# Another order for the pairs of the inverse transform, and the first weight split on GpSimd, in a spectral filter and MLP kernel

## The chip, the cores and the metric

The kernel runs on one core of a Trainium2 chip. The metric is the time of one execution on the device in microseconds (us). A core has TensorE (PE, with PEld for the loads of its stationary operand), VectorE (DVE), ScalarE (ACT), GpSimd (POOL) and SyncE (SP), which issues the DMAs here. Each engine takes its own instructions in program order; semaphores hold an instruction until what it needs is done.

## The reference

A block of a GFNet with an MLP, on 2048 tokens of 576 channels, all in float32:

```python
def _A_ref(x, w_r, w_i):                  # S = 2048, D = 576
    X = jnp.fft.rfft2(x, axes=(-2, -1))
    X = X * (w_r + 1j * w_i)
    return jnp.fft.irfft2(X, s=(S, D), axes=(-2, -1))

def _B_ref(x, w1, w2):                    # w1 576 x 4608, w2 4608 x 576
    h = jnp.maximum(jnp.einsum("bsd,df->bsf", x, w1), 0)
    return jnp.einsum("bsf,fd->bsd", h, w2)

h  = x + _A_ref(layernorm(x), w_r, w_i)
h2 = h + _B_ref(layernorm(h), w1, w2)
```

## The kernel before, in words

The tokens lie in 16 tiles t of 128 rows. The kernel goes through four stages.

1. The forward transform: layer norm (`stat1`, `norm1`), `fold` over the channels, and `fwd_a`, tile after tile.
2. The middle: for 16 groups of frequencies, `mid_d` finishes the forward transform over the channels, `mid_b` transforms over the tokens and multiplies with the filter, `mid_i` begins the way back and writes its result to the buffer `U`. In the middle the first weights of the MLP are read from memory (`load_weights(0)`: a block of `w1` and a block of `w2`).
3. The inverse, interleaved with the first pieces of the MLP. This is the loop over u, a *round* for each pair of tiles, that the change reorders.
4. The main loop: the rest of the MLP as a list of `steps` (g, c), each a group g of 256 hidden units by a chunk c of 4 tiles. From step 8 on the second product is done in Winograd form (`slot`, `prod`, `add`, line 601 and 608).

All products are float32 made of rounded parts: `split` makes a high part h (`act`, a rounding copy on ACT, line 151) and a low part l = v - h (line 307), and a product adds h x h, h x l and l x h. The weights of group 0 go through `split_weights(0, 0)` (`w1`, 1280 columns) and `split_weights(0, 1)` (`w2`, 1152 columns).

The functions of a round, by what they do on which engine:

- `inv_h(u)`: `left` for the two new tiles 2u, 2u+1 (TensorE, into a fresh PSUM buffer each) and `row` for the two old tiles 2u-2, 2u-1 (TensorE, reads `inv_y` in `U`), then line 443 adds the old tiles' result to `xs`, on DVE.
- `inv_d(t)`: four matmuls in `left`'s buffer, an ACT copy into an `e` buffer `ez`, DVE at lines 461 and 462, then the two halves of `inv_y(t)`: line 464 on GpSimd, line 465 on DVE.
- `stat2(t)`: `ln_stats` on the finished tile: lines 208 and 209 on DVE, then for each pair lines 211, 212 and 214 on GpSimd.
- `norm2(t0, 2)`: line 222 on ACT writes the normalized pair `z`.
- `project(t)`: five transposes of `z` on TensorE (lines 483 and 484), two copies on ACT, then the low parts: line 493 on GpSimd, line 494 on DVE. The result goes to the token buffers `xc`, which the MLP's first product reads.
- `unit(k)`: a quarter of an MLP step. Quarters 0 and 1 are `mm1` (first product, 14 matmuls of 512 columns each; after the second, lines 518 and 519 make the split hidden block on ACT and DVE), quarters 2 and 3 are two `mm2` each (second product, 12 matmuls of 288 columns; line 536 adds the result to `xs` on DVE). Units 10 and 11 hold a quarter of step 3's `mm1` as well.

Line 148 is the matmul of nearly all of these, so the profile's rows are told apart by tile names and sizes: `d` is PSUM, `e` the shared buffers, `X` is `U` (later the buffer `tail`), `A` is `xs`, `B`, `C` are `xc`, `D` the hidden blocks.

Nothing schedules this by cost: the order is written out by hand, and each engine follows it. Two shared stocks tie the pieces together beyond their data. There are four PSUM buffers, taken by `left`, `row`, `project`, `mm1` and `mm2` in turn, and ten `e` buffers, taken by `ez`, by `project`, by `z`, by the raw weights (two a group), by the constants `c3t` and by the split weights (two to four a group). A taker gets the buffer that has been free for longest and waits until its last reader is done.

In the order before, round u runs `inv_h(u)`, `norm2` of the pair of round u-2, `inv_d` of pair u, `stat2` of pair u-1, then `project` of the pair just normalized, and in rounds 3 to 8 two units that may read that same pair. `split_weights(0, ...)` stands in rounds 1 and 2.

Of the kernel before, what the change touches and what calls it, by code (L numbers as in the profile page):

```python
# [11 lines left out]
F32R = mybir.dt.float32r  # L12
# [6 lines left out]
NT = 16  # L19
# [102 lines left out]
def dims(ap, off, *pairs):  # L122

    return bass.AP(tensor=ap.tensor, offset=ap.offset + off, ap=[list(ap.ap[0]), *[list(p) for p in pairs]])
# [3 lines left out]
def kernel(ctx: ExitStack, tc: tile.TileContext, x, w_r, w_i, w1, w2, cc2, c1, fb, ib, c3, out):  # L128
    nc = tc.nc
# [3 lines left out]
    def sb(shape, tag, bufs=1, dt=F32):  # L133
        n[0] += 1
        return pool.tile(shape, dt, tag=tag, name=f"{tag}_{n[0]}", bufs=bufs)

    n = [0]

    def ps():
        n[0] += 1  # L140
        return psum.tile([128, 1024], F32, tag="d", name=f"d_{n[0]}", bufs=4)

    def ebuf(shape, dt=F32):
        e = sb([128, EW], "e", EB, dt)[:, :int(np.prod(shape[1:]))]
        return e.rearrange("p (a b) -> p a b", a=shape[1]) if len(shape) == 3 else e

    def mm(o, l, r, start, stop):
        nc.tensor.matmul(o, l, r, start=start, stop=stop)  # L148

    def act(o, i, **kw):  # L150
        nc.scalar.activation(o, i, AF.Copy, **kw)  # L151
# [65 lines left out]
    def ln_apply(xs, t0, k, mvr, zs):  # L217

        r = mvr[2]
        for i in range(k):  # L220
            yield
            nc.scalar.activation(zs[i], xs[:, t0 + i, :], AF.Identity, bias=r[:, 2, i:i + 1], scale=r[:, 1, i:i + 1])  # L222
# [73 lines left out]
    def load_weights(g):  # L296
        v1, v2 = ebuf([128, 5, 256]), ebuf([128, 2, D])
        f = slice(256 * g, 256 * g + 256)
        nc.sync.dma_start(v1[:, 0:4], w1[0:512, f].rearrange("(a p) f -> p a f", p=128))
        for h in range(2):  # L300
            nc.sync.dma_start(v1[64 * h:64 * h + 64, 4], w1[512:576, f])
        nc.sync.dma_start(v2, w2[f, :].rearrange("(a p) d -> p a d", p=128))
        raw[g] = (v1, v2)

    def split(h, l, v):
        act(h, v)
        nc.vector.tensor_sub(l, v, h)  # L307

    pieces = []

    def work(k):
        for _ in range(k):
            split(*pieces.pop(0))

    def split_weights(g, part):
        if g == 1 and part == 0:
            h, l = tail[0][:, 4608:5888], tail[0][:, 5888:7168]
        else:
            h, l = (ebuf([128, (1280, 1152)[part]], F32R) for _ in range(2))
        h, l = (v.rearrange("p (a n) -> p a n", a=(5, 2)[part]) for v in (h, l))  # L320
        wts[g, part] = h, l
        for k in range((5, 2)[part]) if g >= 2 else [slice(None)]:
            pieces.append((h[:, k], l[:, k], raw[g][part][:, k]))
        if g <= 2:
            work(len(pieces))

    tail = []
# [66 lines left out]
    def rows(t, j):  # L394
        k = 64 * (j ^ t % 2)
        return slice(k, k + 64)
# [10 lines left out]
    xc = [xc01[:, 0], xc01[:, 1], xc2]  # L407
    pds, Ez = {}, {}

    def inv_y(t):  # L410
        return U[:, 640 * t:640 * t + D]

    def inv_h(u):

        new = [2 * u, 2 * u + 1] if 2 * u < NT else []
        old = [2 * u - 2, 2 * u - 1] if u else []
        pa = {}

        def left(t):
            pds[t] = ps()  # L420
            for r in range(2):
                for m in range(2):
                    mm(pds[t][64 * m:64 * m + 64, 512 * r:512 * r + 290],
                       U[64 * r:64 * r + 64, 640 * t + 512 + 64 * m:640 * t + 576 + 64 * m], lpv[64 * r:64 * r + 64, r], True, False)

        def row(k):
            for j in range(2):
                for t in old:
                    h = j ^ k
                    mm(pa[t][rows(t, j), 512 * h:512 * h + 288], cai[64 * j:64 * j + 64, 64 * j:64 * j + 64],  # L430
                       inv_y(t)[64 * j:64 * j + 64, 288 * h:288 * h + 288], True, True)

        for t in new[:1]:
            left(t)
        for t in old:
            pa[t] = ps()
        row(0)
        for t in new[1:]:
            left(t)
        row(1)  # L440
        for t in old:
            xt = xs[:, t, :].rearrange("p (h n) -> p h n", h=2)
            nc.vector.tensor_add(xt, xt, pa[t].rearrange("p (h n) -> p h n", h=2)[:, :, :288])  # L443

    def inv_d(t):
        pd = pds.pop(t)
        ut = [dims(U, 640 * t + 128 * b, [1, 128]) for b in range(4)]
        for r in range(2):
            o = pd[:, 512 * r:512 * r + 290]
            for h in range(2):  # L450
                mm(o[:, 145 * h:145 * h + 145], ut[2 * ((r + h) % 2) + r], dev[:, 2 * r + h], False, h == 1)
        if t % 2 == 0:
            Ez[t // 2] = ebuf([128, 4 * 289])
        ez = Ez[t // 2][:, 578 * (t % 2):578 * (t % 2) + 578]
        pdv = pd.rearrange("p (r n) -> p r n", r=2)
        e0, e1 = ez[:, :289], ez[:, 289:578]
        R2 = [289, 2]
        pa_, pb_ = pdv[:, :, 0:145], pdv[:, :, 145:290]
        ea = dims(ez, 0, R2, [1, 145])
        act(ea, pa_)  # L460
        nc.vector.tensor_sub(dims(ez, 288, R2, [-1, 144]), ea[:, :, :144], pb_[:, :, :144])  # L461
        nc.vector.tensor_add(ea, ea, pb_)  # L462
        y = inv_y(t)
        nc.gpsimd.tensor_sub(dims(y, 575, [-1, 287]), e0[:, 1:288], e1[:, 1:288])
        nc.vector.tensor_add(y[:, 0:289], e0, e1)  # L465
# [3 lines left out]
    def stat2(t):  # L469
        t0 = t - t % 2  # L470
        stats[t0] = ln_stats(xs, t0, 2, t % 2, stats.get(t0))

    def norm2(t0, k):
        z = ebuf([128, 2, D])
        for i in range(k):
            Zs[t0 + i] = z[:, i, :]
        return ln_apply(xs, t0, k, stats.pop(t0), [z[:, i, :] for i in range(k)])

    def project(t):
        y = Zs.pop(t)  # L480
        pz = ps()
        for b in range(4):
            nc.tensor.transpose(pz[:, 128 * b:128 * b + 128], y[:, 128 * b:128 * b + 128], ident)  # L483
        nc.tensor.transpose(pz[:, 512:640], y[:, 448:576], ident)
        q = slice(128 * (t % CH), 128 * (t % CH) + 128)
        dst = xc[t // CH]
        pzv = pz.rearrange("p (a s) -> p a s", s=128)
        act(dst[:, 0:5, q], pzv[:, :5])
        if t % 2 == 0:
            Ez[t] = ebuf([128, 1024])  # L490
        zt = Ez[t - t % 2][:, 512 * (t % 2):512 * (t % 2) + 512]
        act(zt, pz[:, :512])
        nc.gpsimd.tensor_sub(dst[:, 5:9, q], zt.rearrange("p (a s) -> p a s", s=128), dst[:, 0:4, q])  # L493
        nc.vector.tensor_sub(dst[0:64, 4, q], pzv[64:128, 4], dst[64:128, 4, q])  # L494
# [65 lines left out]
    def wino_w(*names):  # L560
        for n in names:
            split(*wform(n), fs[n])
# [54 lines left out]
    def slot(i):  # L617
# [16 lines left out]
        add(i, 0, (0, 0))  # L634
        prod(i, "A12", "B21", 1, True)
        split(*fs["S12f"], fs["S12"])
        add(i, 1, (0, 0))
        if w1:
# [41 lines left out]
    def unit(k):  # L680
        i, q = divmod(k, 4)
        if q < 2:
            mm1(i, q)
        else:
            if i == 2:
                mm1(3, q - 2)
            mm2(i, 2 * q - 4)
            mm2(i, 2 * q - 3)

    for u in range(NT // 2 + 2):  # L690
        inv_h(u) if u <= NT // 2 else None
        if 2 <= u:
            for _ in norm2(2 * u - 4, 2):
                pass
        if 2 * u < NT:
            inv_d(2 * u)
            inv_d(2 * u + 1)
        if 1 <= u <= NT // 2:
            stat2(2 * u - 2)
            stat2(2 * u - 1)  # L700
        if u in (1, 2):
            split_weights(0, u - 1)
        if u == 7:
            load_weights(1)
            tail.append(sb([128, 10240], "X", dt=F32R))
            xc.append(tail[0][:, :4608].rearrange("p (a n) -> p a n", a=9))
        if u == 8:
            split_weights(1, 0)
            split_weights(1, 1)
        if u >= 2:  # L710
            project(2 * u - 4)
            project(2 * u - 3)
        if 3 <= u < 9:
            unit(2 * u - 6)
            unit(2 * u - 5)
    for i in range(3, len(steps)):
        if i + 5 < len(steps) and steps[i + 5] == (steps[i + 5][0], 0):
            load_weights(steps[i + 5][0])
# [46 lines left out]
```

## Time and profile before

| | us |
|---|---|
| median of three runs | 1091.26 (1090.89 to 1092.81) |
| the profiled execution | 1092.21 |
| its span, first to last instruction | 1090.1 |
| TensorE busy in the span | 1037.6 (95%) |
| DVE busy | 749.4 (69%) |
| ACT busy | 391.9 (36%) |
| GpSimd busy | 328.7 (30%) |
| mean granted TensorE clock | 0.981 |

The profile is of one execution. A row of the timeline gives start, length, engine, line, operation, what it writes and reads, and in brackets how long the engine stood idle before it and what ended that. A row by stretches gives the stretch, its length, then for PE, PEld, DVE, ACT and POOL the busy time with the number of instructions, then the granted TensorE clock, the busy share of the DMA engines and GB/s. The time of an engine that is not awaited by anyone costs nothing.

### The profile page before, as it was taken

How to read it: one execution, taken by the hardware profiler on the slowest of the kernel's cores; microseconds unless marked ns; L12 is line 12 of the kernel's file. 1: busy time of each engine (PE TensorE's matmuls, PEld its weight loads, DVE VectorE, ACT ScalarE, POOL GpSimd, SP SyncE). 2: the span in 40 equal slices, each digit the busy share in tenths (PEclk: the TensorE clock that was granted, in tenths of full speed). 3: DMA queues.
4: the chain of work that ended last, by engine and by line, in shares of the span. 5: the costliest groups of instructions: out<-in, count | busy, mean ns of one | idle time of the engine just before them, and what ended most of it. 6: DMA issues, size and time to landing. Idle time of an engine off the chain costs nothing.

```text
span 1090.1 us, 17543 instructions
## 1 busy us (share of the span) xinstructions
PE 1037.6 (95%) x6688; PEld 918.6 (84%) x6688; DVE 749.4 (69%) x1411; ACT 391.9 (36%) x894; POOL 328.7 (30%) x436
## 2 busy tenths in 40 slices
PE   8999866969999999999999999999999999999996
PEld 7787545749999999999999999999999999999995
DVE  7587646443447777777777777777777777777765
ACT  4534223232113334333333433333343333334331
POOL 4200244231113243333324323332432333243221
PEclk9999989879999999999999999999999999999998
DMA  9931700101100100000010000001000000100024
GB/s 236 245 78 58 164 1 1 46 12 35 47 20 6 45 24 25 23 25 23 25 46 22 26 22 25 23 25 46 23 26 22 25 23 25 47 23 1 1 71 104
DMA packets 32611, 48.08 MB, mean 44 GB/s; under 512 B 3472, under 2 KB 23184, under 8 KB 32528
## 3 DMA queue, kind: packets, MB, share of 16 engines
q1 hardware_dynamic: 32528, 46.96, 16.0%
q8 instruction: 53, 0.87, 0.3%
q14 instruction: 30, 0.25, 0.1%
HBM read 42.23 MB, written 4.72 MB: 43 GB/s over the span
## 4 chain that ended last, share of the span: by engine, by line
PE 91%; DVE 5%; POOL 2%; ACT 1%; issue 1%; DMA 0%; SPq 0%; DVEq 0%; ACTq 0%; POOLq 0%
PE d L148 58%; PE d L601 32%; DVE st L208 1%; DVE e L462 1%; DVE X L465 1%; DVE e L461 0%; POOL B L493 0%; POOL r L212 0%; ACT e L222 0%; DVE D L519 0%; ACT D L518 0%; DVE mv L209 0%; DMA X<-in_A_x_dram 0%; DVE A L443 0%; PE d L483 0%
## 5 line engine op out<-in xcount | busy, mean ns | idle before, releaser
L608 DVE TENSOR_TENSOR A<-A,d 128x576 f32<-128x576 f32 x448 | 334.6, 747 | 50.1 <-PE d L601 50.0
L601 PE MATMUL d<-X,D 128*128 128x288 f32 x2304 | 346.2, 294 | 1.5 <-DVE A L608 0.9
L601 PEld LDWEIGHTS d<-X,D 128*128 128x128 f32 x2304 | 328.9, 188 | 17.2 <-DVE A L608 1.1
L148 PE MATMUL d<-B,e 128*128 128x512 f32 x952 | 242.4, 396 | 13.8 <-POOL B L493 11.2
L148 PEld LDWEIGHTS d<-B,e 128*128 128x128 f32 x952 | 175.2, 192 | 43.8 <-POOL B L493 11.8
L576 DVE SCALAR_TENSOR_TENSOR D<-d,D 128x256 fp32r<-128x256 f32 x192 | 81.5, 424 | 121.8 <-ACT D L575 121.8
L575 ACT ACTIVATE D<-d 128x256 fp32r<-128x256 f32 x192 | 73.4, 382 | 239.7 <-PE d L148 239.7
L590 POOL TENSOR_TENSOR e<-e 128x256 f32<-128x256 f32 x64 | 47.4, 740 | 355.6 <-ACT e L589 355.6
L148 PE MATMUL d<-C,e 128*128 128x512 f32 x476 | 121.2, 395 | 6.9 <-POOL C L493 5.6
L148 PE MATMUL d<-X,e 128*128 128x512 f32 x476 | 118.8, 390 | 0.0
L151 ACT ACTIVATE X<-e 128x288 fp32r<-128x288 f32 (+2 forms) x177 | 70.2, 434 | 105.6 <-PE d L601 105.6
L307 DVE TENSOR_TENSOR D<-e,D 128x512 fp32r<-128x512 f32 (+1 forms) x128 | 92.7, 724 | 20.0 <-ACT D L151 20.0
L148 PEld LDWEIGHTS d<-C,e 128*128 128x128 f32 x476 | 87.4, 191 | 21.7 <-POOL C L493 5.9
L586 POOL TENSOR_TENSOR e<-e 128x256 f32<-128x256 f32 x64 | 47.5, 742 | 173.4 <-ACT e L585 173.4
L148 PEld LDWEIGHTS d<-X,e 128*128 128x128 f32 x476 | 85.9, 188 | 13.7
L151 ACT ACTIVATE D<-e 128x512 fp32r<-128x512 f32 (+1 forms) x128 | 66.7, 521 | 75.6 <-POOL e L591 71.9
L307 DVE TENSOR_TENSOR X<-e,X 128x288 fp32r<-128x288 f32 (+2 forms) x177 | 83.2, 493 | 0.0
L601 PEld LDWEIGHTS d<-X 128*128 128x128 f32 x384 | 58.0, 188 | 5.1 <-DVE A L608 0.2
L601 PE MATMUL d<-X 128*128 128x288 f32 x384 | 61.4, 295 | 0.0
L519 DVE SCALAR_TENSOR_TENSOR D<-d,D 128x1024 fp32r<-128x1024 f32 x8 | 9.8, 1224 | 65.3 <-ACT D L518 65.3
L148 PE MATMUL d<-e,D 128*128 128x288 f32 x384 | 53.5, 297 | 0.8 <-DVE B L494 0.4
L148 PEld LDWEIGHTS d<-e,D 128*128 128x128 f32 x384 | 52.4, 190 | 1.9 <-DVE B L494 0.6
(79 smaller groups left out, 1015.6 us busy)
## 6 DMA issues: line engine op xcount, KB each, us to landing
e<-in_B_w_dram SPq DMA_DIRECT2D x18, 576.0 KB, 3.8
e<-in_B_w_dram SPq DMA_DIRECT2D x18, 512.0 KB, 3.7
A<-in_A_x_dram SPq DMA_DIRECT2D x16, 288.0 KB, 9.2
out_dram<-A SPq DMA_DIRECT2D x64, 72.0 KB, 2.1
X<-in_A_x_dram SPq DMA_DIRECT2D x12, 288.0 KB, 7.5
e<-in_B_w_dram SPq DMA_DIRECT2D x36, 64.0 KB, 3.5
B<-in_A_w_r_dram SPq DMA_DIRECT2D x15, 144.5 KB, 7.7
B<-in_A_w_i_dram SPq DMA_DIRECT2D x15, 144.5 KB, 7.2
```

Source lines behind the costliest of these rows:

```text
L148: nc.tensor.matmul(o, l, r, start=start, stop=stop)
L151: nc.scalar.activation(o, i, AF.Copy, **kw)
L208: nc.vector.bn_stats(st[:, i, h, :], xs[:, t0 + i, 288 * h:288 * h + 288])
L307: nc.vector.tensor_sub(l, v, h)
L462: nc.vector.tensor_add(ea, ea, pb_)
L465: nc.vector.tensor_add(y[:, 0:289], e0, e1)
L575: nc.scalar.activation(h, p, AF.Relu)
L576: nc.vector.scalar_tensor_tensor(l, p, 0.0, h, op0=ALU.max, op1=ALU.subtract)
L586: nc.gpsimd.tensor_sub(fs["S3"], fs["p0"][:, 0], fs["p0"][:, 1])
L590: nc.gpsimd.tensor_add(fs["S1"], fs["p0"][:, 1], fs["p1"][:, 1])
L601: nc.tensor.matmul(P[:, tt], l[:, q], r, start=first and n_ == 0, stop=n_ == 2, skip_group_check=not first)
L608: nc.vector.tensor_add(xt, xt, P)
```

## The change

Four things are reordered, and one operation moves to another engine. No arithmetic is added or left out.

- The splits of group 0's weights are issued between the middle and round 0, and their low parts are computed by GpSimd instead of DVE. They were in rounds 1 and 2.
- In `inv_h` both `left` stand ahead of all rows; the second stood between the two rows.
- In a round, `project` comes after `inv_d` and takes the pair normalized in the round before (tiles 2u-6, 2u-5, in rounds 3 to 10); `stat2` and then `norm2` follow it. `norm2` stood ahead of `inv_d`, and `project` behind `stat2`. The loop has one round more.
- The units move two rounds on, to rounds 5 to 10, so that a unit reads tokens projected in an earlier round. `load_weights(1)` stays in round 7 but now stands ahead of `project` and `stat2`; `tail` is taken in round 8; the two splits of group 1 fall in rounds 8 and 9 and no longer both in 8.

```diff
-    def split(h, l, v):
+    def split(h, l, v, eng=nc.vector):
         act(h, v)
-        nc.vector.tensor_sub(l, v, h)
+        eng.tensor_sub(l, v, h)
...
-        if g <= 2:
+        if g == 0:
+            split(*pieces.pop(), eng=nc.gpsimd)
+        elif g <= 2:
             work(len(pieces))
...
-        for t in new[:1]:
+        for t in new:
             left(t)
         for t in old:
             pa[t] = ps()
-        row(0)
-        for t in new[1:]:
-            left(t)
-        row(1)
+        for k in range(2):
+            row(k)
...
-    for u in range(NT // 2 + 2):
-        inv_h(u) if u <= NT // 2 else None
-        if 2 <= u:
-            for _ in norm2(2 * u - 4, 2):
-                pass
+    for part in range(2):
+        split_weights(0, part)
+    for u in range(NT // 2 + 3):
+        if u <= NT // 2:
+            inv_h(u)
         if 2 * u < NT:
             inv_d(2 * u)
             inv_d(2 * u + 1)
+        if u == 7:
+            load_weights(1)
+        if u == 8:
+            tail.append(sb([128, 10240], "X", dt=F32R))
+            xc.append(tail[0][:, :4608].rearrange("p (a n) -> p a n", a=9))
+        if 3 <= u:
+            project(2 * u - 6)
+            project(2 * u - 5)
         if 1 <= u <= NT // 2:
             stat2(2 * u - 2)
             stat2(2 * u - 1)
-        if u in (1, 2):
-            split_weights(0, u - 1)
-        if u == 7:
-            load_weights(1)
-            tail.append(sb([128, 10240], "X", dt=F32R))
-            xc.append(tail[0][:, :4608].rearrange("p (a n) -> p a n", a=9))
-        if u == 8:
-            split_weights(1, 0)
-            split_weights(1, 1)
-        if u >= 2:
-            project(2 * u - 4)
-            project(2 * u - 3)
-        if 3 <= u < 9:
-            unit(2 * u - 6)
-            unit(2 * u - 5)
+        if 2 <= u < NT // 2 + 2:
+            for _ in norm2(2 * u - 4, 2):
+                pass
+        if u in (8, 9):
+            split_weights(1, u - 8)
+        if 5 <= u:
+            unit(2 * u - 10)
+            unit(2 * u - 9)
```

## Prediction

> **What bounds the kernel now.** I read the page first, then busy time by stretches, then the waits of TensorE in the stretch that stood out, then the timeline there. From the page, the span and the 40 slices:
>
> ```profile
> span 1090.1 us, 17543 instructions
> PE   8999866969999999999999999999999999999996
> PEclk9999989879999999999999999999999999999998
> ```
>
> TensorE is full from slice 10 on. The holes, and the low clocks, lie in slices 4 to 9, which is the inverse with its interleaved MLP units. Busy time by stretches (us, then each engine's busy time, clock, DMA):
>
> ```profile
> 116.05:127.30 11.25, 9.67 (x89) 6.25 (x89) 5.57 (x12) 2.26 (x5) 2.20 (x3) 1.00 1.05 220
> 134.09:146.80 12.71, 8.26 (x59) 5.39 (x60) 7.95 (x18) 6.54 (x11) 6.71 (x8) 0.87 0.00 0
> 146.80:149.38 2.58, 1.25 (x12) 1.01 (x11) 2.44 (x7) 2.25 (x5) 1.33 (x2) 1.00 0.00 0
> 177.27:182.72 5.45, 5.45 (x59) 4.19 (x58) 3.58 (x7) 1.34 (x3) 0.85 (x2) 1.00 0.00 0
> 182.72:190.16 7.44, 0.50 (x3) 0.19 (x2) 3.58 (x11) 1.77 (x4) 5.31 (x8) 0.73 0.00 0
> 190.16:199.40 9.24, 9.24 (x27) 7.08 (x27) 0.00 (x0) 0.00 (x0) 0.00 (x0) 0.66 0.00 0
> 116.05:257.82 141.77, 106.17 (x721) 82.00 (x721) 69.69 (x146) 43.41 (x69) 47.60 (x62) 0.88 0.16 39
> 257.82:1090.10 832.28, 821.59 (x4835) 745.01 (x4833) 597.21 (x1050) 297.90 (x712) 260.76 (x322) 1.00 0.10 29
> ```
>
> From 116.05 us (first `left`) to 257.82 us (first product of the main loop) TensorE idles 141.77 - 106.17 = 35.6 us, and part of its 106.17 is slow clock: 27 products took 9.24 us at 0.66 where the loop's 28 take 6.47 (below). After 257.82 nothing is left to win: 821.59 of 832.28 is busy. Who held TensorE in the bad stretch (us, times, longest):
>
> ```profile
> PE d L148 <- POOL B L493: 11.2, 2, 5.6
> PE d L148 <- POOL C L493: 5.6, 1, 5.6
> PE d L148 <- DVE X L307: 2.6, 1, 2.6
> ```
>
> L493 writes the last part of a projected token block: three times a pair's first product waits for the projection of its own round. That projection is late because GpSimd first does the statistics (L211 to L214) and because the round's `norm2` stands before it.
>
> **The change, part by part.** I number rounds by u and date each by the first `inv_d` matmul on TensorE. These timeline rows (start, length) show the chain of rounds 1 and 2, then the costs used below:
>
> ```profile
> 114.71 0.90 ACT L151 ACTIVATE X<-d 128x160 f32<-128x160 f32 x4 [2.37 <-PE d L148]
> 118.55 0.41 ACT L151 ACTIVATE e<-d 128x290 f32<-128x290 f32 x1 [2.94 <-PE d L148]
> 121.43 0.90 POOL L464 TENSOR_TENSOR X<-e 128x287 f32<-128x287 f32 x1 [0.45 <-DVE e L462]
> 123.99 2.90 PE L148 MATMUL d<-e,X 128*128 128x145 f32 x24
> 125.73 0.46 DVE L461 TENSOR_TENSOR e<-e,d 128x288 f32<-128x288 f32 x1 [0.63 <-ACT e L151]
> 126.59 1.26 ACT L151 ACTIVATE e<-e 128x1280 fp32r<-128x1280 f32 x1
> 127.32 0.67 PE L148 MATMUL d<-X,cc 64*64 64x288 f32 x2 [0.43 <-DVE X L465]
> 128.06 0.46 DVE L465 TENSOR_TENSOR X<-e 128x289 f32<-128x289 f32 x1
> 128.17 0.90 POOL L464 TENSOR_TENSOR X<-e 128x287 f32<-128x287 f32 x1 [0.45 <-DVE e L462]
> 128.44 0.81 DVE L208 BATCH_NORM_STATS2 st<-A 128x6 f32<-128x288 f32 x2
> 130.21 0.21 DVE L209 BATCH_NORM_AGGREGATE mv<-st 128x2 f32<-128x12 f32 x1
> 130.39 1.49 DVE L307 TENSOR_TENSOR e<-e,e 128x1280 fp32r<-128x1280 f32 x1
> 130.52 1.45 POOL L211 TENSOR_SCALAR r<-mv 128x2 f32<-128x2 f32 x1 [1.44 <-DVE mv L209]
> 130.73 2.25 PE L148 MATMUL d<-e,X 128*128 128x145 f32 x16
> 131.80 1.41 DVE L443 TENSOR_TENSOR A<-A,d 128x576 f32<-128x576 f32 x2
> 135.28 1.16 ACT L151 ACTIVATE e<-e 128x1152 fp32r<-128x1152 f32 x1
> 139.73 1.34 DVE L307 TENSOR_TENSOR e<-e,e 128x1152 fp32r<-128x1152 f32 x1
> 152.88 2.48 POOL L493 TENSOR_TENSOR B<-e,B 128x512 fp32r<-128x512 f32 x2
> 163.37 0.72 PE L148 MATMUL d<-e,X 64*64 64x290 f32 x8
> 163.91 0.67 PE L148 MATMUL d<-X,cc 64*64 64x288 f32 x8
> 164.53 1.22 DVE L519 SCALAR_TENSOR_TENSOR D<-d,D 128x1024 fp32r<-128x1024 f32 x1 [12.61 <-ACT D L518]
> 165.81 0.72 PE L148 MATMUL d<-e,X 64*64 64x290 f32 x8 [1.24 <-DVE D L519]
> 173.54 0.50 DVE L494 TENSOR_TENSOR B<-d,B 64x128 fp32r<-64x128 f32 x2
> 234.53 1.20 PE L148 MATMUL d<-X,cc 64*64 64x288 f32 x16
> 257.82 6.62 PE L148 MATMUL d<-B,X 128*128 128x512 f32 x28
> 264.29 6.54 PE L148 MATMUL d<-e,D 128*128 128x288 f32 x48
> ```
>
> *First weights split at the middle's end.* Two ACT copies (1.26 and 1.16) start after the middle's last copy, at 114.71 + 0.90 = 115.6, and end at 118.0, inside the 2.94 us for which ACT waited before 118.55: nothing. DVE loses its two L307 (1.49 and 1.34). GpSimd gains two subtractions, which no row shows at this size; nearest is L493, 2.48 for two of 512 columns, 1.24 each. Scaled by columns that is 3.1 + 2.8 = 5.9; with a start-up share taken out, as L464's 0.90 for 287 suggests (0.34 for 225 more columns, 1.5 ns each), 2.4 + 2.2 = 4.6. I take 5.5, nearer the rows of like type. They run from 116.9 to 122.4, and both L464 of round 0 are queued behind them: the second ends at 122.4 + 1.8 = 124.2 where it ended at 122.33. So 1.9 us later, between 1.0 and 2.3. If DVE's L465 (both operands in SBUF) shuts GpSimd out, as L307 did to L211 (1.45 for two columns, ending at 131.97, just after L307), two times 0.46 come on top; if it is DVE that is held, about as much.
>
> [...]
>
> *Both `left` ahead of the rows.* From the end of the second L464 (128.17 + 0.90 = 129.07) to `inv_d` at 130.73 are 1.66 us; the second `left` in it takes 163.91 - 163.37 = 0.54, and now lies in the idle time before. So 1.12 remains. All four PSUM buffers are then taken in the order left, left, row, row: behind a unit of first products, the one that waits for L519 is the second row instead of the second `left` (1.24 before; I take 1.3, between 0 and 1.8).
>
> *Rounds 1 to 4, now without units.* Round 1: 124.2 + 1.1 = 125.3 (before 123.99). From `inv_d` to the end of the second L464 are 129.07 - 123.99 = 5.08, so a round takes 5.08 + 1.12 = 6.2 by that chain. DVE needs 1.42 (L443) + 2.79 (125.73 to 128.52) + 1.97 (128.44 to 130.42) = 6.2, and with the projection's L494 (0.50) 6.7. GpSimd needs less than the 6.71 of 134.09:146.80, which is one round of it with an L211 held by the L307 that goes; its statistics now stand behind L493, but only the next round's `norm2` needs them. ACT's `norm2` no longer stands before the next `ez` copies. Rounds: 125.3, 131.5, 137.7, 144.1, 150.8. Round 3 to 4 is a mean of the two pitches.
>
> *Rounds 5 to 10: TensorE full.* Every unit reads tokens projected a round earlier (L493 of round 4 ends at 150.8 - 1.12 + 2.48 = 152.2, the first product starts at 154), every transpose a `norm2` of the round before. A full round is 5.45 of inverse work (2.10 of it before `inv_d`) and 6.47 of first products or 6.38 of second (257.82 to 264.29, and to 270.67). DVE then needs at most 6.7 + 4 x 0.75 = 9.7 in 11.9: covered. Ends:
> - 5: 150.8 + 3.35 + 6.47 = 160.6
> - 6: + 5.45 + 1.3 (L519) + 6.38 = 173.7
> - 7: + 5.45 + 6.47 = 185.6
> - 8: + 1.20 rows + 1.25 project + 6.38 + 0.6 = 195.0; the 0.6 is the second projection's PSUM buffer, which L519 frees late
> - 9: + 1.25 + 6.47 + 0.4 = 203.1; the 0.4 is a buffer freed by the second products' add, behind L307 of group 1
> - 10: + 1.25 + 12.85 = 217.2
>
> The main loop starts at 217.2 instead of 257.82: 40.6 us earlier, of which 1.3 us was given to GpSimd's split. Moving the four weight DMAs of `load_weights(1)` within round 7 costs nothing: SyncE's queue holds nothing else there, and the `e` buffers they take come free in round 6; if they came two rounds late, the split in round 8 would wait. The two splits of group 1 (ACT 1.26 and 1.16, DVE 1.49 and 1.34) now fall in rounds 8 and 9, not both before the first product that needs them; that wait of 2.6 (L307) goes.
>
> The profiled execution took 1092.21, its span 1090.1, and the median of the three runs is 0.95 lower. 1092.21 - 40.6 = 1051.6, less 0.95 is 1050.7. I say **1051**.
>
> **Rivals.**
>
> *The bare rounds cool TensorE (1058).* The clock fell where it idled: 0.87 in 134.09:146.80 (65% busy), 0.66 behind an idle stretch of 5.6. Rounds 1 to 4 fill 4.2 to 5.5 of 6.2 to 6.7. For: that is not full. Against: 116.05:127.30 held 1.00 at 86%, and no wait in rounds 1 to 4 is longer than about 1.3. Price: at 0.75 the 3.2 us of TensorE in each chain grow by 1.1, four times, and the first 27 products by up to 9.24 - 6.24 = 3.0: 7 us.
>
> [...]
>
> *The wait moves to the statistics (1066).* They are queued behind L493 now; if `norm2` were late by those 2.48 in each of rounds 5 to 10, 15 us come back. For: in round 3 the products waited for just this queue, the other way round. Against: `norm2` has a round of 11.9 us to be done.
>
> *It doesn't do what it says (1075).* If a unit waited for any projection into its buffer, rounds 5 and 7 would keep waiting 5.6 each and cool after it, and 9 too: 3 x (5.6 + 2.4) = 24. Against: the rows of a pair's first block start at 127.32, before the second block's L465 and L464 write the same buffer, so regions are told apart.
>
> *Slower (1096).* Weight halves hold four `e` buffers from 116 on, `c3` one, and `z` now lives across rounds: four are left for three takes a round. If each take waited for the round before to end, rounds would run one after the other, at 12.71 + 0.5 as in 134.09:146.80. Eleven of these are 145 instead of 141.77, 4 us slower; it decides from 12.9 a round. Against: each slot is taken again a round or more after its last reader.
>
> **How the numbers follow.** Forecast 0.66, cool rounds 0.18, statistics 0.09, unchanged waits 0.04, slower 0.03. The forecast's own span is 1046 (no stalls in rounds 6 to 9, GpSimd quick) to 1056; with the cooling rival the range is 1046 to 1064, which leaves out some 0.16. About 0.2% is what a measurement can tell from no change: faster 0.96, same 0.01, slower 0.03.
>
> **What would show it.** After: no TensorE wait on L493; L464 of round 0 near 124; `inv_d` pitch 6 to 7 us four times; TensorE full from about 150; the main loop's first product near 217; clock 1.00 throughout. Wrong if the clock dips in rounds 1 to 5, if transposes wait for L222, or if the loop after 217 no longer takes 832 us.

## The result, and the profile after

| | before | after |
|---|---|---|
| median of six executions each, us | 1092.61 | 1054.49 (1052.18 to 1055.34) |
| ratio of the times | | 0.965, 95% interval 0.9636 to 0.9664 |
| profiled execution, us | 1092.21 | 1052.18 |
| its span, us | 1090.1 | 1050.3 |

The kernel is 38 us faster; the forecast was 1051, within 1046 to 1064. The page of the changed kernel, span and slices:

```profile
span 1050.3 us, 17539 instructions
PE   8999899999999999999999999999999999999995
PEclk9999999999999999999999999999999999999998
```

Of the dent in slices 4 to 9 only the 8 in slice 4 is left, which holds round 0; the low clocks there are gone. Busy time by stretches (stretch, length, then PE, PEld, DVE, ACT, POOL, clock, DMA), cut at the first `inv_d` of rounds 1, 2 and 3, then rounds 5 and 6, then the sums that answer to those of before:

```profile
116.04:125.74 9.70, 6.77 (x66) 3.96 (x65) 5.29 (x7) 2.58 (x4) 7.25 (x4) 1.00 1.05 222
125.74:131.99 6.25, 5.57 (x50) 3.45 (x49) 5.39 (x14) 0.83 (x2) 1.80 (x2) 1.00 0.55 117
131.99:138.24 6.25, 5.57 (x50) 3.44 (x49) 5.76 (x15) 2.34 (x4) 3.25 (x6) 1.00 0.00 0
151.57:161.38 9.81, 9.81 (x57) 8.28 (x54) 7.21 (x19) 4.62 (x8) 8.50 (x14) 1.00 0.01 3
161.38:174.60 13.22, 12.45 (x107) 10.76 (x106) 9.90 (x20) 5.64 (x9) 5.77 (x8) 1.00 0.31 92
116.04:217.56 101.52, 94.93 (x721) 75.00 (x721) 69.59 (x145) 44.97 (x72) 52.84 (x66) 1.00 0.22 54
217.56:1050.30 832.74, 821.49 (x4834) 744.99 (x4832) 597.26 (x1049) 296.03 (x708) 258.13 (x320) 1.00 0.10 29
```

The main loop is as long as before (832.74 against 832.28). The stretch ahead of it shrank from 141.77 to 101.52: its idle time from 35.6 to 6.6 us, its busy time from 106.17 to 94.93 for the same 721 matmuls, at a clock of 1.00 instead of 0.88. What TensorE still waits for there (us, times, longest):

```profile
PE d L148 <- DVE X L465: 4.3, 4, 2.2
PE d L148 <- DVE e L462: 1.0, 2, 0.6
PE d L148 <- DVE D L519: 0.8, 1, 0.8
PE d L483 <- DVE D L519: 0.5, 1, 0.5
```

No wait on L493 is left. The longest one is new: 2.2 us in round 0, for DVE's L465. The timeline there, and the main loop's first product:

```profile
116.88 5.48 POOL L307 TENSOR_TENSOR e<-e,e 128x1280 fp32r<-128x1280 f32 x2 [75.08 <-DMA A<-in_A_x_dram]
118.92 0.46 DVE L461 TENSOR_TENSOR e<-e,d 128x288 f32<-128x288 f32 x1 [5.10 <-ACT e L151]
119.90 2.77 DVE L465 TENSOR_TENSOR X<-e 128x289 f32<-128x289 f32 x1
122.31 0.91 POOL L464 TENSOR_TENSOR X<-e 128x287 f32<-128x287 f32 x1
122.82 0.67 PE L148 MATMUL d<-X,cc 64*64 64x288 f32 x2 [2.25 <-DVE X L465]
125.74 3.39 PE L148 MATMUL d<-e,X 128*128 128x145 f32 x32
217.56 4.72 PE L148 MATMUL d<-B,X 128*128 128x512 f32 x20
```

L465, 0.46 us everywhere else, lasts 2.77 and ends 0.3 after GpSimd's two subtractions (116.88 + 5.48 = 122.36). L461, which reads one operand from PSUM, takes its usual 0.46 beside them.

### The profile page after: what moved, and what is told of

It is laid out like the page before. It is cut to its first block, busy times and chain, and to the rows that moved or that the text cites. A ratio compares the mean times of both kernels' runs of the same rounds, so it can differ in the third digit from the quotient of the medians.

```text
span 1050.3 us, 17539 instructions
## 1 busy us (share of the span) xinstructions
PE 1026.7 (98%) x6688; PEld 912.0 (87%) x6688; DVE 749.3 (71%) x1409; ACT 392.2 (37%) x894; POOL 331.2 (32%) x438
## 4 chain that ended last, share of the span: by engine, by line
PE 93%; DVE 3%; ACT 1%; POOL 1%; issue 0%; DMA 0%; SPq 0%; ACTq 0%; DVEq 0%; POOLq 0%
PE d L148 59%; PE d L601 34%; PE d L483 1%; DVE X L465 1%; DVE e L462 0%; DVE e L461 0%; DVE st L208 0%; ACT e L222 0%; DMA X<-in_A_x_dram 0%; POOL r L212 0%; POOL B L493 0%; DVE D L519 0%; ACT D L518 0%; DVE e L362 0%; ACT e L151 0%
## 5 line engine op out<-in xcount | busy, mean ns | idle before, releaser
L148 PE MATMUL d<-B,e 128*128 128x512 f32 x952 | 237.3, 390 | 0.0
L148 PEld LDWEIGHTS d<-B,e 128*128 128x128 f32 x952 | 171.9, 188 | 27.8 <-issue 0.2
L148 PE MATMUL d<-C,e 128*128 128x512 f32 x476 | 118.9, 390 | 0.0
L307 DVE TENSOR_TENSOR D<-e,D 128x512 fp32r<-128x512 f32 (+1 forms) x128 | 92.7, 724 | 20.1 <-ACT D L151 20.1
L307 DVE TENSOR_TENSOR X<-e,X 128x288 fp32r<-128x288 f32 (+2 forms) x177 | 83.2, 493 | 0.3 <-POOL r L211 0.3
L591 POOL TENSOR_TENSOR e<-e,e 128x256 f32<-128x256 f32 x64 | 50.5, 789 | 5.0
```

Source lines behind the costliest of these rows:

```text
L307: eng.tensor_sub(l, v, h)
L591: nc.gpsimd.tensor_sub(fs["S2"], fs["S1"], fs["p0"][:, 0])
```

## The experiments

The theory: the units' distance from the projection, and the order on ACT and GpSimd in the bare rounds, carry the gain; the split costs a little. The rivals are named with each run. Each kernel was timed beside the kernel before (medians 1091.6 to 1092.5); I compare medians with the changed kernel's 1054.49 and, where it was run again, 1054.13.

**Units back to their own pair.** Nothing else is undone.

```diff
-        if 5 <= u:
-            unit(2 * u - 10)
-            unit(2 * u - 9)
+        if 4 <= u < NT // 2 + 2:
+            unit(2 * u - 8)
+            unit(2 * u - 7)
```

> The changed kernel with the units one round earlier (rounds 4 to 9), so that a unit again reads tokens projected in its own round; projection still three pairs back. Theory A (the distance of the units carries the gain): in rounds 4, 6 and 8 the first product waits for L493, which ends some 4.5 us after the transposes, and TensorE cools after it (2 us each), less 1.3 for a fuller round 4: 3 x 6.5 - 1.3 = 18 us slower than the changed kernel, 1072. Rival B (the order on GpSimd and ACT carries it: L493 ahead of the statistics, norm2 behind the copies): waits under 2 us without cooling, 1057.

Measured: 1070.45 us (1068.45 to 1071.81), 16 slower. TensorE's waits, the products of round 4, and the clock after their wait:

```profile
PE d L148 <- POOL B L493: 5.4, 2, 2.9
PE d L148 <- ACT B L151: 2.7, 2, 1.3
PE d L148 <- POOL C L493: 1.5, 1, 1.5
PE d L148 <- ACT C L151: 1.3, 1, 1.3
152.99 8.03 PE L148 MATMUL d<-B,e 128*128 128x512 f32 x27 [2.87 <-POOL B L493]
153.16:156.57 3.41, 3.41 (x9) 2.62 (x10) 0.00 (x0) 0.00 (x0) 1.31 (x4) 0.51 0.00 0
```

Theory A holds. The waits of these four rows are 10.9 us, in the three rounds where a unit reads its own pair. In round 4 a window of 3.4 us behind them runs at half clock (0.51 above), and the 27 products behind each of the three take 8.03, 8.02 and 8.04 where 6.24 is usual (27/28 of the loop's 6.47): 5.4 in all. Together 16.3, the difference of the two profiled executions (1068.45 and 1052.18). The waits on L493 are shorter than the 5.6 of before. That L493 now stands ahead of the statistics, as Rival B had it, can explain some 1.6 us of it, which is what GpSimd spends on them in round 3 of the changed kernel (138.51 to 140.14); where the rest comes from no run separates. Rival B was wrong that waits under 2 us leave the clock alone: in round 8 they are 1.3 and 1.5 us, with one product between, and the 27 products take 8.04 all the same.

**Only the units moved, in the kernel before.**

```diff
-        if 3 <= u < 9:
-            unit(2 * u - 6)
-            unit(2 * u - 5)
+        if 4 <= u:
+            unit(2 * u - 8)
+            unit(2 * u - 7)
```

> The kernel before with one edit: the units one round later (rounds 4 to 9), so that they read tokens projected a round earlier. Projection, splits, left and row stay as before. Theory A: the waits on L493 (16.8 us), on the copies before them (4) and most of the slow clock (8) go, the slow rounds 2 to 4 stay: main loop from about 224, 1060 to 1064. Rival B: without the other order the wait moves to the transposes, which need L222 behind the statistics, 3 to 4 us a round: 1075.

Measured: 1064.53 us (ratio 0.9749, 0.9735 to 0.9764), 28 faster than before, just past the late end of theory A. TensorE's waits, its first units and the main loop:

```profile
PE d L148 <- DVE B L494: 5.8, 3, 3.2
PE d L483 <- ACT e L222: 3.0, 2, 1.9
157.81 6.63 PE L148 MATMUL d<-B,e 128*128 128x512 f32 x28
230.34 4.95 PE L148 MATMUL d<-B,X 128*128 128x512 f32 x21
```

No wait on L493, and the first 28 products take 6.63 us (6.62 in the loop before). The bare rounds 3 and 4 stay slow, behind L494 and L222: `inv_d` of round 4 starts 9.9 us later than in the changed kernel (154.71 against 144.85), and the main loop 12.8. Part of the rest is one more wait for L222, 1.9 us ahead of unit 10, whose first 14 products then take 5.04 us where 3.36 is usual. The rival was half right: transposes do wait for L222, but 3.0 us in all, not 3 to 4 a round.

**The projection back in the round of its `norm2`.**

```diff
             inv_h(u)
+        if 2 <= u < NT // 2 + 2:
+            for _ in norm2(2 * u - 4, 2):
+                pass
         if 2 * u < NT:
...
-        if 3 <= u:
-            project(2 * u - 6)
-            project(2 * u - 5)
+        if 2 <= u < NT // 2 + 2:
+            project(2 * u - 4)
+            project(2 * u - 3)
...
-        if 2 <= u < NT // 2 + 2:
-            for _ in norm2(2 * u - 4, 2):
-                pass
```

> The changed kernel with norm2 ahead of inv_d again and the projection in the round of its norm2 (rounds 2 to 9), units where the change has them (now two pairs behind). Theory A: from round 5 on nothing waits, but in rounds 2 to 4 ACT's two L222 (1.63 us, waiting for GpSimd's statistics) stand before the ez copies that the round's chain needs: 2.2 to 3 us a round, 1054.5 + 8 = 1062. Rival B (only the units' distance counts): 1054.5.

Measured: 1065.68 us (1064.15 to 1066.56), 11 slower than the changed kernel where I had 8. Two waits and the first `inv_d` of rounds 3, 4 and 5:

```profile
PE d L483 <- ACT e L222: 5.2, 5, 1.5
ACT e L222 <- POOL r L214: 9.9, 2, 5.0
142.85 2.25 PE L148 MATMUL d<-e,X 128*128 128x145 f32 x16
152.21 2.25 PE L148 MATMUL d<-e,X 128*128 128x145 f32 x16
162.57 3.19 PE L148 MATMUL d<-e,X 128*128 128x145 f32 x16
157.70:164.50 6.80, 6.27 (x40) 3.67 (x41) 5.86 (x15) 1.85 (x5) 5.65 (x8) 0.50 0.00 0
```

The place is as expected, rounds 2 to 4: a pitch of 9.4 from round 3 to 4 where the changed kernel has 6.6. The clock then fell for 6.8 us, which I had not counted. From round 5 to 7 the projection waits for nothing, though it stands in the same round as its `norm2`; in rounds 8 and 9 it waits 0.7 and 1.2 us for L222 again, so "from round 5 on nothing waits" was not quite right. Rival B, that only the units' distance counts, is off by 11 us.

The parts overlap. The units' move alone is worth 28, everything but it 22 (1092.46 - 1070.45), both 38: some 12 us go with either of them.

**The split back in rounds 1 and 2**, on DVE, and **at the middle's end on DVE**.

```diff
-        if g == 0:
-            split(*pieces.pop(), eng=nc.gpsimd)
-        elif g <= 2:
+        if g <= 2:                       # both kernels
...
-    for part in range(2):                # split_r12 only
-        split_weights(0, part)
...
             stat2(2 * u - 1)
+        if u in (1, 2):                  # split_r12 only
+            split_weights(0, u - 1)
```

> The changed kernel with the splits where they were before, on DVE in rounds 1 and 2, behind stat2. Theory A: round 0 is as quick as before the change (inv_d of round 1 at 123.5, 2.2 us earlier), but rounds 1 and 2, where DVE needs 6.2 us of a round of 6.25, grow by 1.4 each: sum +0.6, 1055.1. Rival: DVE has slack there and this is 2.2 us faster, 1052.3.

> The changed kernel with the splits at the same place, low parts on DVE instead of GpSimd. Theory A: DVE is idle there (5.1 us before its first L461); its two L307 end at about 119.5, so L461 of round 0 is late by 0.6, nothing is held, and inv_d of round 1 starts at 124.1: 1.6 us faster than the changed kernel, 1052.9. Rival: the move to GpSimd is what takes load off DVE and pays; then this is slower by up to the 2.8 us that DVE gets back, 1057.

Measured: in rounds 1 and 2 1052.18 us (1051.93 to 1052.52), at the middle's end on DVE 1050.83 (1050.64 to 1050.96). Both beat the changed kernel: by 2 us where the splits were before, by 3.3 on DVE at the new place. The first `inv_d` of rounds 1 to 4 tells why, of `split_r12` and then round 1 of `split_dve`:

```profile
123.55 3.39 PE L148 MATMUL d<-e,X 128*128 128x145 f32 x32
129.80 3.75 PE L148 MATMUL d<-e,X 128*128 128x145 f32 x32
137.19 2.25 PE L148 MATMUL d<-e,X 128*128 128x145 f32 x16
144.35 2.25 PE L148 MATMUL d<-e,X 128*128 128x145 f32 x16
124.37 3.39 PE L148 MATMUL d<-e,X 128*128 128x145 f32 x32
```

In `split_r12` round 1 is 2.2 us earlier than in the changed kernel. Its two L307, behind the statistics of rounds 1 and 2, make the next pitches 7.39 instead of 6.25 and 7.16 instead of 6.61; at round 4 it is still 0.5 ahead. My expectation had them at 1.4 each, which is theirs on DVE, while 1.1 and 0.5 reached the path. So the rounds give 0.5, and the rival's 1052.3 is met for another reason; the rest of the 2 us goes with the clock, below. `split_dve` gains 1.4 in round 0, near the 1.6 expected, and also more by the clock.

**The split one step earlier**, on GpSimd (`split_mid`, run twice) and on DVE (`mid_dve`).

```diff
             mid_i(i - 2)
+        if i == NP:
+            for part in range(2):
+                split_weights(0, part)
...
-    for part in range(2):
-        split_weights(0, part)
     for u in range(NT // 2 + 3):
```

`mid_dve` has the edit of `split_dve` as well.

> The changed kernel with the two splits of group 0 issued one step earlier, behind the last but one mid_i, still on GpSimd. Theory A: GpSimd is done by about 119, DVE's L465 of round 0 (2.77 us in the changed kernel) takes 0.46 again, inv_d of round 1 starts at 123.5 instead of 125.7, all later rounds 2.2 us earlier: 1052.3. If the hole of 2.25 us in round 0 is also what lets the clock fall, all executions lie at 1050. Rival: GpSimd now holds DVE's L361 and L362 at the middle's end (both operands in SBUF) and the last mid_i is late by as much: no gain, 1054.5, or up to 1 us slower.

> The kernel of split_mid once more, beside the two below on one chip. Theory A: 1050.3, executions within 1 us of each other, since round 0 has no hole of 2.25 us in which the clock could fall. Rival: the narrow spread was chance, and executions reach 1053.

> The splits in the middle, as in split_mid, with the low parts on DVE instead of GpSimd. Theory A: DVE idles from 114.3 to 119.4 there, the two L307 (2.8 us) fit, nothing is held: the same as split_mid, 1050.3 within 0.5; which engine computes the low parts is worth nothing there, only when. Rival: GpSimd's part in it pays, and this is slower by 1 us or more.

Measured: 1050.29 us (1049.78 to 1050.64) and again 1050.21 (1049.61 to 1050.60); on DVE 1050.03 (1049.80 to 1050.23). In `split_mid`, GpSimd's pair, L465 (line 468 in this kernel) and round 1:

```profile
114.04 5.58 POOL L307 TENSOR_TENSOR e<-e,e 128x1280 fp32r<-128x1280 f32 x2 [72.22 <-ACT e L151]
120.35 0.46 DVE L468 TENSOR_TENSOR X<-e 128x289 f32<-128x289 f32 x1
123.87 3.39 PE L148 MATMUL d<-e,X 128*128 128x145 f32 x32
```

L465 is back to 0.46 and round 1 starts 1.9 us earlier. The hold did not move to the middle: its last L362, which begins at 113.81, 0.2 us ahead of GpSimd's pair, stays at 0.46. The second run has the same narrow spread, so that was not chance of one run. GpSimd or DVE makes no difference there, 0.2 us with the ranges overlapping: what counts is when. These are the fastest kernels of the study, 4 us ahead of the change as made; `mid_dve` has ratio 0.9618 (0.9604 to 0.9631) to before.

**Why 4 and not 2.2: the clock.** The changed kernel's executions lie at 1052.2 (clock 0.997) or from 1054.0 to 1055.3 (0.991 to 0.996), those of `split_mid`, `split_dve` and `split_r12` within 1 us each. The mean clock of an execution doesn't say where it fell, so the place has to be read from a profile: the profiled `split_mid` has 0.995 with a clock of 1.00 in round 0 (116.48 to 123.87 us) and the usual 3.39, 1.64 and 2.25 us for the products of rounds 1 to 5. Its first `left` starts 0.4 us later than in the changed kernel's profile (116.48 against 116.04); where its low clock lies was not shown.

> The changed kernel once more, for its spread. Theory A (the order of the work): time 1052 to 1055 as measured, median about 1054.5. The 2 to 3 us between its faster executions (granted clock 0.997) and the others (0.991 to 0.995) are then TensorE windows at half clock, two or three of them; a profile of such an execution should show them in rounds 0 to 4 (116 to 152 us), where TensorE is not full. Rival B: they lie elsewhere (the start, or the main loop), and have nothing to do with the rounds.

Measured: 1054.13 us (1053.99 to 1055.13). The profile fell on one of the later kind. Stretches around round 1, and three rows of the timeline:

```profile
116.10:122.89 6.79, 4.53 (x50) 3.10 (x49) 3.84 (x4) 2.58 (x4) 5.95 (x3) 1.00 1.05 221
124.70:128.11 3.41, 3.41 (x17) 2.16 (x16) 1.51 (x2) 0.00 (x0) 0.00 (x0) 0.50 1.04 222
124.23 2.64 PE L148 MATMUL d<-X,cc 64*64 64x288 f32 x14 [0.68 <-DVE X L465]
126.81 4.00 PE L148 MATMUL d<-e,X 128*128 128x145 f32 x32
133.66 3.39 PE L148 MATMUL d<-e,X 128*128 128x145 f32 x32
```

One window of 3.4 us at half clock, right after round 0's hole: the 14 row matmuls take 2.64 instead of 1.64, and round 2 starts at 133.66 instead of 131.99. That is 1.7 of the 1.8 us between the two profiled executions (1052.18 and 1054.02). My expectation had two or three such windows; this execution has one in the rounds. Whether the hole does it, or GpSimd, a kernel without GpSimd in that place tells. It is `split_dve` with work repeated on DVE, so that DVE is late by itself:

```diff
         eng.tensor_sub(l, v, h)
+        last[:] = [l, v, h]
+
+    last = []
...
-    for part in range(2):
-        split_weights(0, part)
+    split_weights(0, 0)
+    l, v, h = last                       # the operands of that split
+    split_weights(0, 1)
+    nc.vector.tensor_sub(l, v, h)
+    nc.vector.tensor_sub(l[:, 0], v[:, 0], h[:, 0])
```

> The kernel of split_dve (1050.8, hole in round 0 0.47 us) with the low part of the first weights computed once more on DVE, and 256 of its columns a third time (1.49 + 0.42 us): no GpSimd, but a hole of about 2.4 us at the same place as in the changed kernel. Theory A (the hole lets the clock fall in some executions): 1052.7 in the best, median near 1054, executions 2 us or more apart. Rival B (GpSimd's operation does it): 1052.7, all within 0.6.

Measured: 1054.85 us (1054.37 to 1055.22).

```profile
123.36 0.67 PE L148 MATMUL d<-X,cc 64*64 64x288 f32 x2 [2.33 <-DVE X L466]
124.10:130.90 6.80, 6.19 (x29) 4.75 (x30) 2.69 (x5) 0.41 (x1) 0.90 (x1) 0.50 0.83 177
```

The hole alone brings the clock down, to 0.50 for 6.8 us here. The median is theory A's; the spread is not: none of the four executions stayed at 1052.7. That the other three dipped in the rounds too is read from their mean clock, 0.992 or 0.993 where all four of `split_dve` have 0.995.

**Both `left` ahead**, undone on top of `split_mid`, so that the clock doesn't blur it.

```diff
-        for t in new:
+        for t in new[:1]:
             left(t)
         for t in old:
             pa[t] = ps()
-        for k in range(2):
-            row(k)
+        row(0)
+        for t in new[1:]:
+            left(t)
+        row(1)
```

> The splits issued in the middle (as in split_mid, 1050.3), and the second left back between the rows. Theory A: 0.54 us a round on the path in rounds 1 and 2, which the chain through L464 sets, less in 3 and 4, which DVE sets: 1051.5. Rival: left is hidden either way, 1050.3.

Measured: 1052.01 us (1051.66 to 1052.31), 1.7 slower than `split_mid`. From round 1 to 2:

```profile
124.07 2.90 PE L148 MATMUL d<-e,X 128*128 128x145 f32 x24
130.81 2.90 PE L148 MATMUL d<-e,X 128*128 128x145 f32 x24
```

A pitch of 6.74 against 6.26 (123.87 to 130.13) in `split_mid`: half a microsecond a round, as the 0.54 of the prediction. Round 2 loses as much, and so does round 0, which I had left out (7.88 us from the first `left` to `inv_d` of round 1, against 7.39); rounds 3 and 4 lose a quarter each. The main loop starts 1.7 later, counted from the first `left`.

**The split alone, in the kernel before** (the two `split` edits and the place, nothing else of the change).

> The kernel before with the split part of the change alone: the splits at the middle's end, low parts on GpSimd. Theory A: round 0 is held by 2.2 us as in the changed kernel; in rounds 1 and 2 DVE is relieved of 1.49 and 1.34, of which the second was on the path (the wait of 3.2 us on L494 behind it): +2.2 - 1.3 = 0.9 slower, 1092.5. Rival: both were on the path, 0.6 faster, 1091.

Measured: 1093.48 us (1091.02 to 1095.61), ratio 1.0014 (1.0004 to 1.0025). TensorE's waits, first two rows of the kernel before, then the same two here:

```profile
PE d L148 <- DVE X L465: 2.3, 4, 0.7
PE d L148 <- DVE B L494: 3.6, 2, 3.2
PE d L148 <- DVE X L467: 4.5, 4, 2.7
PE d L148 <- DVE B L496: 2.4, 2, 2.0
```

The wait for L465 (here line 467) rises from 2.3 to 4.5, the one on L494 (line 496) falls from 3.6 to 2.4. Also in the kernel before, this part of the change is a small loss: 1.8 us by the medians where I had 0.9, between 0.4 and 2.7 by the interval. Behind the hole the last 14 row matmuls and the `left` among them take 3.20 us in this profile (124.85 to `inv_d` at 128.05), where the kernel before takes 2.06 (121.93 to 123.99); that was not in my sum.

## Why the prediction was right

The steps, against the profiled execution without a dip in its clock:

| step | predicted | measured |
|---|---|---|
| `inv_d` of round 1 | 125.3 | 125.74 |
| rounds 2, 3, 4, 5 | 131.5, 137.7, 144.1, 150.8 | 131.99, 138.24, 144.85, 151.57 |
| end of rounds 5 and 6 | 160.6, 173.7 | 161.38, 174.60 |
| end of rounds 7, 8, 9 | 185.6, 195.0, 203.1 | 186.38, 196.03, 203.71 |
| main loop starts | 217.2 | 217.56 |
| profiled execution | 1051.6 | 1052.18 |

- *Rounds 5 to 10 full*: right. What TensorE still waits for in rounds 6 and 8 is L519, 0.8 and 0.5 us. The wait of 0.4 that I put into round 9, behind L307 of group 1, is not there.
- *The bare rounds at 6.2, then 6.7*: right, 6.25, 6.25, 6.61, 6.72. DVE's sum told round 4, the chain through L464 rounds 1 and 2. TensorE was busy for 5.57 to 6.28 us of each, more than the 4.2 to 5.5 that the cooling rival was argued with, and its longest wait there is 0.7, not 1.3.
- *The split*: sized well enough for round 1 (0.4 us off), with the wrong branch of the mechanism. I had GpSimd held by DVE, or DVE by about 0.9; DVE was held for 2.3, until GpSimd had finished. Its two subtractions took 5.48 against my 5.5. The near match is partly luck: my sum queued both L464 back to back behind the subtractions and had the second end at 124.2; it ended at 124.57 by another path, L465 held, then L461, L462 and the second L464 in turn. I gave the split 1.3 us; what I did not draw is that this is more than it saves, even against DVE in rounds 1 and 2, and that half clock can follow the wait it makes (2.26 us in `after_again`).
- *Clock 1.00 throughout*: so in the profiled execution; not in most others, if the profile of `after_again` stands for them. There the clock falls to 0.50 for 3.4 us behind the wait of 2.26 that the split makes in round 0, and the low window reaches into round 1, so a sign that I had named as proving me wrong did come. It costs about 2 us, not the rival's 7, and it comes from another place: the bare rounds, whose fill the rival blamed, keep 1.00 in the profiled execution, with 5.57 of 6.25 us busy in rounds 1 and 2.
- *From the profile to the median*: I took 0.95 off, as the runs of before had it. After the change the profiled execution is among the fastest, without a dip, and 2.3 below the median. So 3.2 of the 3.5 us between 1051 and 1054.49 lie here, and 0.6 in the steps above, less 0.3 of rounding.

The other rivals did not come: no transpose waits for L222, no first product for its own round, and nothing that TensorE waits for points to an `e` buffer.

## What to carry to other kernels

Read a hole in the bounding engine by what its own round asks of the other engines: a consumer moved one round behind its producer takes the whole chain off the path, if the buffers reach. Cost each part of a change by itself; here parts worth some 40 us hid one that lost 2 (4 against the best place found for it), and the better place for it was a step earlier, where both engines were idle. Before giving work to GpSimd, look for DVE operations with both operands in SBUF that fall into the same time, as L465 did here (2.77 us instead of 0.46).

## What the runs showed of the hardware

- L465, a DVE operation with both operands in SBUF, lasted until GpSimd's subtractions beside it had ended (2.77 us instead of 0.46, to 122.67, the subtractions to 122.36); L461, with an operand in PSUM, didn't (0.46 beside the same pair of subtractions). The profile counts the hold as busy time. Before the change L211 on GpSimd came up behind L307 on DVE and took 1.45 us instead of 0.23, to 131.97, where L307 ended at 131.88. Both times the second was held for about all that was left of the first.
- A wait of 2.25 to 2.33 us of TensorE in round 0, in a stretch of about 6.8 us with 4.53 busy, was followed by half clock in three of the five profiled executions that have it: 0.50 for 3.4 us in `after_again`, 0.50 for 6.8 us in `dve_hole`, and in `norm_ahead` by its times (14 row matmuls took 2.63 us and the 32 of `inv_d` 4.93, where 1.64 and 3.39 are usual). In the changed kernel's first profile the clock stayed at 1.00, and in `units_own` the same products took 1.64 and 3.39. The longest single wait does not tell the cases apart: in `norm_ahead` the clock fell again, to 0.50 for 6.8 us from 157.7, where no wait was above 1.5 and TensorE had been busy for some 1.7 of the last 3.4 us, while a single wait of 1.24 us with 5.44 of 6.68 busy (163.37 to 170.05 before the change) left it at 1.00.
